# Moving one 512 KB load from ahead of a job's rows to behind its weights

## The chip, the cores and the metric

The kernel runs on one core of a Trainium2 chip. The metric is the device time of one execution in microseconds (us), and several runs are compared by their median. A core has TensorE for matmuls (PE, with PEld for its weight loads), VectorE (DVE), ScalarE (ACT), GpSimd (POOL) and SyncE (SP), which only issues transfers and reads registers. All transfers of the core share 16 DMA engines; those that SP issues go through one queue of the profile (q1), the indirect ones that POOL issues through another (q0).

## The reference

A retention layer (linear attention with a decay per head) over 4 batches of 768 tokens, 8 heads of 64, then a mixture of 8 experts, where each token goes to the one expert with the largest gate value:

```python
for t in range(S):
    state = gamma * state + k[:, :, t] (outer) v[:, :, t]
    y[:, :, t] = scale * q[:, :, t] @ state
x = y as 3072 rows of 512
logits = x @ w_gate + modality_bias[modality_id]
e_idx = argmax(logits); gate_w = softmax(logits)[e_idx]
for e in range(8):                      # 512 -> 1024 -> 512, relu between
    out[rows of e] = gate_w * (relu(x[rows of e] @ w1[e]) @ w2[e])
```

All inputs and the output are float32.

## The kernel before

The retention part is cut into 24 chunks of 128 tokens (`NN`), numbered 0 to 23. A chunk needs two transfers of 512 KB: `kq` (keys and queries by feature, `load_kq`, L114) and `kv` (keys and values by token, `load_kv`, L120). Chunks below `WHOLE = 9` are computed in one piece (`whole_scores`, `whole_state`, `whole_out`), later ones in two halves (`quarters`). For each chunk POOL multiplies the values by decay factors (`decay_v`, L1059, tile `vd`); PE adds keys times `vd` to a running state (`st`; `grown` in the later chunks, all recorded at L276), and forms the output `y` from the scores `sc`. `tokens_out` (L388) then gives the rows `x` of the expert layer and their gate values.

Rows are routed in groups of three chunks. When a group is routed, POOL scatters its rows (`x_dram<-xs,pos`, L494, three indirect transfers, one per chunk) into lists by expert in DRAM. From the lists come jobs: a job is 256 rows of one expert. The kernel begins its first job before most chunks are done: after group 1 (chunks 3, 4 and 5). `start_job` reads the place of the job's rows from a small list (L986), and `load_rows` brings them in as `xg` (L838, two transfers of 257 KB), which wait for the scatters of the groups that may hold the job's rows. PE transposes them (`flip_x`, `xp`, L857), ACT and DVE split them and the weights `raw` into high and low parts (`hi`, `lo`, L813 and L815), and PE multiplies (`h`, L872, then `o`, L887), three products for one. The 10 jobs that begin before the routing is complete have an `e` in their names. The weights of the first job are loaded early for a guessed expert; L809 loads them again only if the guess was wrong, and the second matrix follows at L807.

The order of work on PE, ACT, DVE and SP is that in which the Python code emits it (`manual_schedule`): each engine runs its own instructions in that order and waits where an input or a buffer isn't ready. `retention` is a generator that emits one step at a time, and `everything` puts the jobs' steps between its steps. SP therefore issues its transfers one after the other; one that has to wait holds up all that stand behind it. The pool for `kv` has three buffers beside four borrowed ones: chunk 11 takes the buffer of chunk 8, chunk 12 that of chunk 9.

Of the kernel before, what the change touches and what calls it, by code (L numbers as in the profile page):

```python
# [41 lines left out]
WHOLE = 9  # L42
# [13 lines left out]
def kernel(  # L56
# [43 lines left out]
    def room(kind, n, bufs):  # L100
        shape, name = [P, 2, DM], f"{kind}_{n}"
        if (kind, n) in lent:
            return me.tile(shape, F32, tag=lent[kind, n], name=name)
        if kind == "kq":
            return fours[free.index(n) % 4].rearrange("p (a b) -> p a b", a=2)
        return ld.tile(shape, F32, tag=kind, name=name, bufs=bufs)
# [9 lines left out]
    def load_kv(n):  # L116
        if n in kvs or n >= NN:
            return
        t = kvs[n] = room("kv", n, 3)
        nc.sync.dma_start(t, qkv[n][:, 2:4])  # L120
# [33 lines left out]
    def setup_a():  # L154
        nc.vector.tensor_copy(wgt[:, :, :P], ident.unsqueeze(1).to_broadcast([P, NG, P]))
        nc.vector.memset(ones, 1.0)
        nc.vector.memset(cnt[0], 0.0)
# [53 lines left out]
    def scores(n):  # L211
        p = psc[n] = bank(f"sc_{n}").rearrange("p (u g t) -> p u g t", u=2, g=NG)
        kt, qt = feat(n, 0), feat(n, 1)
        return [
            (p[rows(j), u, g], kt[rows(j), g, rows(u)], qt[rows(j), g, rows(u)], True)
            for u in range(2) for g in range(NG) for j in range(2)
        ]

    def masked(n):
        att[n] = wk.tile([P, 2, NG, D], F32, tag="a", name=f"a_{n}")  # L220
        nc.vector.tensor_tensor(
            att[n].rearrange("p u g t -> p (u g) t"),
            psc.pop(n).rearrange("p u g t -> p (u g) t"),
            half.unsqueeze(1).to_broadcast([P, H, D]), op=ALU.mult,
        )
# [47 lines left out]
    def run(*lists):  # L273
        for i in range(0, max([0] + [len(l) for l in lists]), 2):
            for out_, l, r, start in sum((l[i : i + 2] for l in lists), []):
                nc.tensor.matmul(out_, l, r, start=start, stop=True, skip_group_check=True)  # L276
# [4 lines left out]
    def whole_scores(n):  # L281
        kt, qt = feat(n, 0), feat(n, 1)
        p = [bank(f"sc{j}_{n}").rearrange("p (g t) -> p g t", g=NG) for j in range(2)]
        for g in range(NG):
            for j in range(2):
                nc.tensor.matmul(
                    p[j][:, g], kt[rows(j), g], qt[rows(j), g], start=True, stop=True,
                    skip_group_check=True,
                )
        psc[n] = p  # L290

    def whole_masked(n):
        p = psc.pop(n)
        att[n] = me.tile([P, 2, NG, P], F32, tag=f"hi1{2 + n % 2}", name=f"a_{n}")
        for j in range(2):
            nc.vector.tensor_tensor(
                att[n][:, j], p[j], mask.unsqueeze(1).to_broadcast([P, NG, P]), op=ALU.mult
            )

    def whole_state(n):  # L300
        c = n % NCH
        if c == 0:
            pst[n // NCH] = bank(f"st_{n}")[:, : NG * D].rearrange("p (g e) -> p g e", g=NG)
        p = pst[n // NCH]
        kk = kvs[n][:, 0].rearrange("p (h d) -> p h d", h=H)
        for g in range(NG):
            for j in range(2):
                nc.tensor.matmul(
                    p[rows(j), g], kk[:, 2 * g + j], vds[n][:, 2 * g + j],
                    start=(c == 0 and g == 0), stop=True, skip_group_check=True,  # L310
                )
        keep_state(n + 1, 0)
        if c == NCH - 2 and n + 1 < WHOLE:
            pst.pop(n // NCH)
# [66 lines left out]
    def tokens_out(n, yT):  # L381
        xs = xrows[n] = wk.tile([P, ROW], F32, tag="xs", name=f"xs_{n}", bufs=6)
        lh = wk.tile([P, H, NE], F32, tag="lh", name=f"lh_{n}")
        c = n % NCH
        for u in range(2):
            px = bank(f"x_{n}_{u}")[:, : 2 * XW].rearrange("p (b e) -> p b e", b=2)
            for g in range(2):
                nc.tensor.matmul(  # L388
                    px[:, g], yT[:, 2 * u + g], wgt[:, 2 * u + g], start=(g == 0), stop=(g == 1),
                    skip_group_check=True,  # L390
                )
            hs = slice(4 * u, 4 * u + 4)

            def gained(out_, src, w):
                shape = [P, 2, 2, w]
                nc.vector.tensor_tensor(  # L396
                    out_.rearrange("p (b j) w -> p b j w", b=2),
                    src.rearrange("p b (j w) -> p b j w", j=2),
                    gain[:, c, hs].rearrange("p (b j) -> p b j", b=2).unsqueeze(3)
                    .to_broadcast(shape),  # L400
                    op=ALU.mult,
                )

            gained(lh[:, hs], px[:, :, P:], NE)
            x = xs[:, u * 2 * P : (u + 1) * 2 * P].rearrange("p (h d) -> p h d", h=4)
            if u == 0:
                gained(x, px[:, :, :P], D)
            else:
                for i in range(4):
                    nc.scalar.activation(  # L410
                        x[:, i], px[:, i // 2, rows(i % 2)], AF.Copy,
                        scale=gain[:, c, 4 * u + i : 4 * u + i + 1],
                    )
        gr = n // GRP
        if n % GRP == 0:
            lg[gr] = sm.tile([P, GRP, NE], F32, tag="lg", name=f"lg_{gr}")
        nc.vector.tensor_reduce(
            lg[gr][:, n % GRP], lh.rearrange("p h e -> p e h"), axis=AX.X, op=ALU.add
        )
# [635 lines left out]
    def decay_v(n):  # L1055
        vv = kvs[n][:, 1].rearrange("p (h e) -> p h e", h=H)
        by = decw if n < WHOLE else dec
        vds[n] = wk.tile([P, H, D], F32, tag="vd", name=f"vd_{n}", bufs=3)
        ins = nc.gpsimd.tensor_tensor(  # L1059
            vds[n], vv, by[:, n % NCH].unsqueeze(2).to_broadcast([P, H, D]), op=ALU.mult  # L1060
        )
        vd_last[:] = [getattr(ins, "ins", ins)]
        if held and n >= WHOLE:
            held.pop(0)()
# [88 lines left out]
    def retention(modi):  # L1153
        whole_scores(0)
        whole_masked(0)
        decay_v(1)
        setup_a()
        prev = None
        for n in range(NN):
            if n < WHOLE:  # L1160
                if (n + 1) % NCH:
                    whole_state(n)

                load_kv(n + 7 if n < 3 else n + 3)
                listed = n == (min(EVENTS) + 1) * GRP
                if listed:

                    tokens_out(*prev)
                    route(min(EVENTS))
                if n + 1 < WHOLE:  # L1170
                    whole_scores(n + 1)
                else:
                    run(scores(n + 1))
                    if (n + 1) % NCH:
                        hand_over(n + 1)

                yield n
                if n + 1 < WHOLE:
                    whole_masked(n + 1)
                else:  # L1180
                    masked(n + 1)
                if prev is not None and not listed:
                    tokens_out(*prev)
                    if n % GRP == 0:
                        route(n // GRP - 1)
                if n + 1 == WHOLE:
                    run(grown(n + 1, 0))
                    keep_state(n + 1, 1)
                if not listed:
                    yield n  # L1190
                prev = None
                yT = whole_out(n)
            else:
                yT = yield from quarters(n)
                if n + 1 < NN:
                    masked(n + 1)
                load_kv(n + 3)
            if n + 2 < NN:
                decay_v(n + 2)
            load_kq(n + 8 if n < 4 else n + 4)  # L1200
            if n == 0:
                setup_b(modi)
            elif n == 1:
                list_consts()
            if prev is not None:
                tokens_out(*prev)
                if n % GRP == 0:
                    route(n // GRP - 1)
            prev = (n, yT)
            yield n  # L1210
        tokens_out(*prev)
        route(NGRP - 1)
        yield NN
# [172 lines left out]
```

## Time and profile before

| | us |
|---|---|
| Median of 3 runs | 418.19 (418.08 to 419.0) |
| The profiled execution | 419.12 |
| Its span, first to last instruction | 417.3 |
| PE busy in the span | 398.5 (95%) |
| PE weight loads, DVE, ACT, POOL busy | 349.3, 251.6, 207.3, 90.6 |

The profile shows one execution, instruction by instruction, with times from the span's start; some 1.8 us of the execution lie around the span. Where PE is busy nearly all the time, what counts is the few places where it waits, and the place of any delay: one that PE meets while it has nothing else to do lengthens the program.

### The profile page before, as it was taken

How to read it: one execution, taken by the hardware profiler on the slowest of the kernel's cores; microseconds unless marked ns; L12 is line 12 of the kernel's file. 1: busy time of each engine (PE TensorE's matmuls, PEld its weight loads, DVE VectorE, ACT ScalarE, POOL GpSimd, SP SyncE). 2: the span in 40 equal slices, each digit the busy share in tenths (PEclk: the TensorE clock that was granted, in tenths of full speed). 3: DMA queues.
4: the chain of work that ended last, by engine and by line, in shares of the span. 5: the costliest groups of instructions: out<-in, count | busy, mean ns of one | idle time of the engine just before them, and what ended most of it. 6: DMA issues, size and time to landing. Idle time of an engine off the chain costs nothing.

```text
span 417.3 us, 11996 instructions
## 1 busy us (share of the span) xinstructions
PE 398.5 (95%) x4598; PEld 349.3 (84%) x4598; DVE 251.6 (60%) x605; ACT 207.3 (50%) x420; POOL 90.6 (22%) x118
## 2 busy tenths in 40 slices
PE   3999859999999999999999999999999999999993
PEld 3888759889979988988988988979898998878852
DVE  1777847855654767547855855967665673725600
ACT  1235347456645554556446547536554655536411
POOL 2426310233132124112501231310230101002001
PEclk9999989999999999999999999999999999999998
DMA  8999659979887764536940414842287688998001
GB/s 278 392 413 357 183 161 373 361 255 337 268 294 264 273 229 130 174 91 217 300 134 37 144 50 153 248 157 78 78 276 257 207 276 309 347 409 336 2 2 44
DMA packets 29978, 92.78 MB, mean 222 GB/s; under 512 B 4827, under 2 KB 4955, under 8 KB 29857
## 3 DMA queue, kind: packets, MB, share of 16 engines
q1 hardware_dynamic: 25360, 77.83, 54.3%
q0 software_dynamic: 4272, 13.67, 8.5%
q8 instruction: 37, 0.61, 0.6%
q10 hardware_dynamic: 288, 0.50, 0.4%
q14 instruction: 21, 0.17, 0.1%
HBM read 92.74 MB, written 17.48 MB: 264 GB/s over the span
## 4 chain that ended last, share of the span: by engine, by line
PE 65%; issue 16%; DMA 4%; DVE 2%; POOL 2%; POOLq 1%; ACT 1%; SPq 0%; ACTq 0%
PE h_e L872 25%; PE o_e L887 24%; PE x L388 5%; PE sc L276 3%; PE st L276 3%; PE xp_e L857 2%; PE y L276 2%; DMA x_dram<-xs,pos 2%; POOL out_dram L900 1%; DMA raw<-in_w_dram 1%; DMA xg_e<-x_dram 1%; DVE lo_e L815 1%; DMA four<-in_w_dram 1%; ACT hi_e L813 1%; POOL out_dram L974 0%
## 5 line engine op out<-in xcount | busy, mean ns | idle before, releaser
L815 DVE TENSOR_TENSOR lo_e<-raw,hi_e 128x1024 fp32r<-128x1024 f32 x80 | 100.1, 1253 | 75.9 <-ACT hi_e L813 75.4
L872 PE MATMUL h_e<-xTh,hi_e 128*128 128x256 f32 x320 | 91.9, 287 | 0.0
L872 PE MATMUL h_e<-xTh,lo_e 128*128 128x256 f32 x320 | 90.3, 282 | 0.0
L872 PE MATMUL h_e<-xTl,hi_e 128*128 128x256 f32 x320 | 90.3, 282 | 0.0
L813 ACT CAST hi_e<-raw 128x1024 fp32r<-128x1024 f32 x80 | 83.7, 1047 | 4.4 <-DMA raw<-in_w_dram 4.4
L887 PE MATMUL o_e<-hi_e,hTh 128*128 128x512 f32 x160 | 66.1, 413 | 0.0
L887 PE MATMUL o_e<-lo_e,hTh 128*128 128x512 f32 x160 | 63.2, 395 | 0.0
L887 PE MATMUL o_e<-hi_e,hTl 128*128 128x512 f32 x160 | 63.0, 394 | 0.0
L872 PEld LDWEIGHTS h_e<-xTh,hi_e 128*128 128x128 f32 x320 | 60.7, 190 | 0.7
L872 PEld LDWEIGHTS h_e<-xTh,lo_e 128*128 128x128 f32 x320 | 60.6, 189 | 0.3
L872 PEld LDWEIGHTS h_e<-xTl,hi_e 128*128 128x128 f32 x320 | 60.7, 190 | 0.0
L1059 POOL TENSOR_TENSOR vd<-kv,cst 128x512 f32<-128x512 f32 x24 | 26.3, 1098 | 102.8 <-PE y L276 39.3
L822 ACT ACTIVATE hTh<-h_e 128x256 fp32r<-128x256 f32 x80 | 30.8, 388 | 29.7 <-PE h_e L872 26.1
L410 ACT ACTIVATE xs<-x,cst 128x64 f32<-128x64 f32 x96 | 22.3, 316 | 45.2 <-DVE lh L396 26.6
L900 POOL DMA_INDIRECT out_dram<-o_e,xg_e x20 | 19.8, 988 | 111.2 <-ACT o_e L899 94.9
L823 DVE SCALAR_TENSOR_TENSOR hTl<-h_e,hTh 128x256 fp32r<-128x256 f32 x80 | 33.0, 418 | 13.7 <-ACT hTh L822 13.6
L887 PEld LDWEIGHTS o_e<-lo_e,hTh 128*128 128x128 f32 x160 | 30.1, 188 | 7.0
L887 PEld LDWEIGHTS o_e<-hi_e,hTh 128*128 128x128 f32 x160 | 30.1, 188 | 6.1
L494 POOL DMA_INDIRECT x_dram<-xs,pos x24 | 27.8, 1157 | 34.1 <-DVE xs L460 12.7
L899 ACT ACTIVATE o_e<-o_e,xg_e 128x512 f32<-128x512 f32 x20 | 13.8, 690 | 42.8 <-issue 27.9
L887 PEld LDWEIGHTS o_e<-hi_e,hTl 128*128 128x128 f32 x160 | 30.2, 189 | 5.5
L815 DVE TENSOR_TENSOR lo_s<-raw,hi_s 128x1024 fp32r<-128x1024 f32 x16 | 19.6, 1222 | 21.0 <-ACT hi_s L813 21.0
(214 smaller groups left out, 670.9 us busy)
## 6 DMA issues: line engine op xcount, KB each, us to landing
raw<-in_w_dram SPq DMA_DIRECT2D x100, 512.0 KB
kv<-in_qkv_dram SPq DMA_DIRECT2D x24, 512.0 KB
four<-in_qkv_dram SPq DMA_DIRECT2D x19, 512.0 KB
xg_e<-x_dram SPq DMA_DIRECT2D x20, 257.0 KB
four<-in_w_dram SPq DMA_DIRECT2D x8, 512.0 KB
wb_u<-in_w_dram SPq DMA_DIRECT2D x16, 256.0 KB
kq<-in_qkv_dram SPq DMA_DIRECT2D x4, 512.0 KB
xg_s<-x_dram SPq DMA_DIRECT2D x4, 257.0 KB
```

Of the source, the lines that this page charges most:

```text
L276: nc.tensor.matmul(out_, l, r, start=start, stop=True, skip_group_check=True)
L388: nc.tensor.matmul(px[:, g], yT[:, 2 * u + g], wgt[:, 2 * u + g], start=(g == 0), stop=(g == 1), skip_group_check=True,)
L410: nc.scalar.activation(x[:, i], px[:, i // 2, rows(i % 2)], AF.Copy, scale=gain[:, c, 4 * u + i : 4 * u + i + 1],)
L494: ins = nc.gpsimd.indirect_dma_start(out=x_dram[:, :], out_offset=bass.IndirectOffsetOnAxis(ap=pos[:, i : i + 1], axis=0), in_=xs, in_offs ...
L813: nc.scalar.copy(hi, raws[m][i])
L815: nc.vector.tensor_tensor(lo, raws[m][i], hi.bitcast(F32), op=ALU.subtract)
L822: nc.scalar.activation(hi, src, AF.Relu)
L823: nc.vector.scalar_tensor_tensor(lo, src, 0.0, hi.bitcast(F32), op0=ALU.max, op1=ALU.subtract)
L872: nc.tensor.matmul(ph, s["w1"][f // 2][wi][:, o : o + P], s["xT"][kc // 2][a][:, kc % 2, :], start=(n == 0), stop=(n == 3 * KC - 1),)
L887: nc.tensor.matmul(po, hT[f][a][:, hh * P : (hh + 1) * P], s["w2"][f // 2][wi][:, (f % 2) * DM : (f % 2 + 1) * DM], start=(n == 0), stop=( ...
L900: ins = nc.gpsimd.indirect_dma_start(out=out[:, :], out_offset=bass.IndirectOffsetOnAxis(ap=xg.bitcast(I32)[:, DM : DM + 1], axis=0), in_= ...
L1059: ins = nc.gpsimd.tensor_tensor(vds[n], vv, by[:, n % NCH].unsqueeze(2).to_broadcast([P, H, D]), op=ALU.mult)
```

## The change

```diff
@@ retention, chunks in one piece
-                load_kv(n + 7 if n < 3 else n + 3)
+                if n + 1 < WHOLE:
+                    load_kv(n + 7 if n < 3 else n + 3)
@@ retention, chunks in halves
                 yT = yield from quarters(n)
                 if n + 1 < NN:
                     masked(n + 1)
+
+                if n == WHOLE:
+                    load_kv(n + 2)
                 load_kv(n + 3)
```

With `n = 8` the old code issued the `kv` load of chunk 11 (the twelfth, as they are counted from 0). The new code leaves it out there and issues it with `n = 9`, just ahead of that of chunk 12. In between the code emits the first job's start: the read of its list, its rows and its weights. Nothing else is added or removed.

On SP, around the first job's start, `kv_11` stood ahead of the reads of the list `lst1` and of the job's rows `xg0` and `xg1`; the last number of a name is only a buffer's number, and `e10` is the first job. Before:

```order
L807 DMA raw13_105<-in_w1_dram 128x1024
L120 DMA kv_10_694<-in_qkv_dram 128x1024
L120 DMA kv_11_815<-in_qkv_dram 128x1024
L986 TENSOR_LOAD lst1_850
...
L838 DMA xg0_e10_875<-x_dram_75 128x514
```

After:

```order
L807 DMA raw13_105<-in_w1_dram 128x1024
L120 DMA kv_10_694<-in_qkv_dram 128x1024
L986 TENSOR_LOAD lst1_848
...
L838 DMA xg0_e10_873<-x_dram_75 128x514
```

The load of chunk 11 no longer stands ahead of the rows. Further on in SP's order, behind the first job's second weight matrix (`raw20` to `raw23`), before:

```order
L807 DMA raw23_109<-in_w2_dram 128x1024
L114 DMA four_76<-in_qkv_dram 128x1024
L120 DMA kv_12_1049<-in_qkv_dram 128x1024
L114 DMA four_76<-in_qkv_dram 128x1024
L986 TENSOR_LOAD lst1_850
```

After:

```order
L807 DMA raw23_109<-in_w2_dram 128x1024
L114 DMA four_76<-in_qkv_dram 128x1024
L120 DMA kv_11_1047<-in_qkv_dram 128x1024
L120 DMA kv_12_1049<-in_qkv_dram 128x1024
L114 DMA four_76<-in_qkv_dram 128x1024
L986 TENSOR_LOAD lst1_848
```

It now stands where the load of chunk 12 stood, and that load and all behind it come one transfer later; `four` is the buffer of `kq`.

On POOL, which waits for `kv_11`, the order is the same in both kernels. Here it is in the new one, with the three scatters of group 1 (`pos_1`) ahead of the decays:

```order
L494 DMA x_dram_75<-xs_3_496,pos_1_720 24704x514
L494 DMA x_dram_75<-xs_4_573,pos_1_720 24704x514
L494 DMA x_dram_75<-xs_5_623,pos_1_720 24704x514
L1059 TENSOR_TENSOR vd_10_948<-kv_10_694,cst_77 128x512
L1059 TENSOR_TENSOR vd_11_1051<-kv_11_1047,cst_77 128x512
L1059 TENSOR_TENSOR vd_12_1298<-kv_12_1049,cst_77 128x512
```

`vd_11` keeps its place between `vd_10` and `vd_12`. PE's order is also the same in both; it first uses `vd_11` and `kv_11` in the second half of chunk 10, between two parts of the first job:

```order
L276 MATMUL sc_11_1130<-four_76 64x64 x2
L276 MATMUL y_10_1129<-a_10_1045,vd_10_948 64x64 x2
L276 MATMUL st_9_832<-vd_11_1051,kv_11_1047 64x64 x2
L276 MATMUL y_10_1129<-a_10_1045,vd_10_948 64x64 x2
L276 MATMUL st_9_832<-vd_11_1051,kv_11_1047 64x64 x2
```

Nothing moved there, but its input `kv_11` is now issued later.

## The prediction

> **What bounds the kernel now.** I read first who waits for whom, for PE alone: in the whole run there are three waits that matter.
>
> ```profile
> PE sc L286 <- DMA four<-in_qkv_dram: 5.4, 1, 5.4
> PE xp_e L857 <- DMA xg_e<-x_dram: 4.2, 2, 3.2
> PE st L344 <- ACT s L271: 1.1, 1, 1.1
> ```
>
> The columns are total us, times, longest. The first is the start of the program. The second, 4.2 us, is PE waiting for the rows of the first job. Then the busy time by stretch (length, then busy us of PE, PEld, DVE, ACT, POOL, then PE clock, DMA share, GB/s):
>
> ```profile
> 53.00:63.00 10.00, 5.82 (x109) 5.07 (x102) 5.07 (x9) 4.74 (x10) 0.39 (x1) 0.83 0.59 180
> 63.00:100.00 37.00, 37.00 (x559) 33.24 (x558) 26.12 (x62) 22.46 (x46) 10.09 (x10) 1.00 0.92 325
> ...
> 300.00:400.00 100.00, 100.00 (x692) 86.56 (x691) 55.03 (x75) 52.38 (x83) 11.97 (x12) 1.00 0.72 255
> ```
>
> From 63 to 400 us PE has no gap, so what PE wins by 63 us is kept to the end unless a new wait appears; and what it loses isn't won back. The chain of waits through the gap:
>
> ```profile
> 46.65 6.94 DMA x_dram<-xs,pos
> 53.60 0.35 SPq L838
> ...
> 54.17 3.62 DMA xg_e<-x_dram
> 57.83 1.45 PE xp_e L857 x7
> ```
>
> The third scatter of group 1, issued at 46.65, lands only at 53.60; until then SP can't issue the rows, and these take 3.6 us more. SP had come to that wait at 50.6 (first row), 3.0 us earlier (second row):
>
> ```profile
> L838 SPq MOVE xg_e<-x_dram x2: 29/29/29, 50.6 to 54.1; - x2
> SPq L838 <- DMA x_dram<-xs,pos: 3.0, 1, 3.0
> ```
>
> So the scatter's landing, not SP, sets the end of the gap. The load that moves was issued in the midst of the scatters:
>
> ```profile
> 44.05 1.01 POOL L494 DMA_INDIRECT x_dram<-xs,pos  x1 [2.95 <-DVE key L662]
> 45.37 0.97 POOL L494 DMA_INDIRECT x_dram<-xs,pos  x1 [0.30 <-issue]
> 46.65 0.98 POOL L494 DMA_INDIRECT x_dram<-xs,pos  x1 [0.30 <-issue]
> L120 SPq DMA_DIRECT2D kv<-in_qkv_dram x1: 339/339/339, 45.8 to 45.8; - x1
> 46.50:48.00 1.50, 0.41 (x14) 0.27 (x12) 1.43 (x4) 1.36 (x6) 1.35 (x2) 1.00 1.00 52
> 48.00:49.50 1.50, 1.31 (x23) 1.14 (x24) 1.16 (x5) 0.37 (x1) 0.70 (x1) 1.00 0.75 284
> 49.50:51.00 1.50, 1.50 (x38) 1.34 (x36) 1.34 (x5) 0.35 (x2) 0.00 (x0) 1.00 0.89 354
> 51.00:53.50 2.50, 2.35 (x90) 1.88 (x80) 0.00 (x0) 0.84 (x4) 1.04 (x1) 1.00 0.05 16
> ```
>
> From 46.5 to 49.5 us, 1.5 x 52 + 1.5 x 284 GB/s = 0.50 MB moved: just the 0.52 MB of the load. The next 1.5 us carry 0.53 MB, what two scatters of 257 KB amount to. So scatters two and three went behind the load. The first scatter, ahead of it, landed after 4.4 us; the 24 scatters of the run range from 3.2 to 8.4:
>
> ```profile
> DMA to landing us min/median/max: 4.4/4.4/4.4
> DMA to landing us min/median/max: 3.2/5.9/8.4
> ```
>
> **Gain: the rows come earlier.** One transfer of 512 KB leaves the DMA engines at 46.5 to 49.5 us. By how much the third scatter lands sooner, call it G, no row shows; the bounds are these. From above, SP isn't ready before 50.66, so G is at most 53.60 - 50.66 = 2.94. From below 0, if the landing hangs on something else. Between lie two rows. If the third scatter lands like the first, at 46.65 + 4.4 = 51.05, G is 2.55. If only the time that the load needs at the best rate is saved, 0.524 MB / 418 GB/s (row of 68 to 71 us below), G is 1.25. That lower value has a reason of its own: in this stretch the instruction queue has one packet, and its share is large.
>
> ```profile
> q8 instruction: 1, 0.02, 5.2%
> ```
>
> 5.2% of 16 engines over 46.5 to 50 us is 0.052 x 16 x 3.5 = 2.9 us: one DMA engine was held by one instruction fetch, and its part of the scatters ends last with or without the load. I take the middle of 1.25 and 2.55, G = 1.9.
>
> The Trainium skill, page "DMA: Bandwidth & Descriptors", section "Queues, rings and completion order", says that a DMA engine takes turns between queues by whole packets of some 9 to 17 descriptors; the order of bytes above agrees. The same page, section "Anatomy of one DMA — SWDGE (gpsimd) path", puts the fixed cost at about 2.0 us and adds bytes at 436 GB/s, an estimate of 2.6 us for a scatter; the trace has 4.4 at its place, and by the page's figure the rows would wait only for SP (G = 2.94).
>
> **Cost: chunk 11 comes later.** The load now stands where that of chunk 12 stood, the sixth of those that SP issues without condition behind the rows (four of weights, one `kq`), and the wait moves to POOL's `vd`:
>
> ```profile
> 52.35 1.04 POOL L1059 TENSOR_TENSOR vd<-kv,cst 128x512 f32<-128x512 f32 x1 [3.65 <-PE y L328]
> 70.59 1.04 POOL L1059 TENSOR_TENSOR vd<-kv,cst 128x512 f32<-128x512 f32 x1 [17.20 <-DMA kv<-in_qkv_dram]
> 58.11 1.95 SPq L807 DMA_DIRECT2D raw<-in_w_dram  x4
> 60.15 0.52 SPq L114 DMA_DIRECT2D four<-in_qkv_dram  x1
> 60.78 0.40 SPq L120 DMA_DIRECT2D kv<-in_qkv_dram  x1
> 71.49 0.23 PE L276 MATMUL st<-vd,kv 64*64 64x64 f32 x2
> ```
>
> The first row is `vd_11`, done at 53.4, 18 us before PE uses it at 71.49 (last row). The second is `vd_12`, which begins at 70.59, when its load, issued at 60.78, has landed. In the new kernel `vd_11` takes that place: SP's whole sequence from the rows on is earlier by G, so it begins at 70.59 - G and ends 1.04 later; with 0.1 for the signal PE can go on at 71.73 - G. Without this wait PE would come there at 71.49 - G or sooner. So this costs at least 0.24, and whatever PE wins above G there is lost again. All other engines only follow.
>
> PE can win above G, since its clock fell:
>
> ```profile
> 58.00:59.20 1.20, 1.20 (x7) 0.88 (x6) 0.93 (x2) 1.20 (x3) 0.00 (x0) 0.58 0.07 10
> 59.20:62.30 3.10, 3.10 (x72) 2.98 (x72) 2.75 (x6) 1.65 (x4) 0.00 (x0) 0.61 0.97 330
> ...
> 68.00:71.00 3.00, 3.00 (x30) 2.87 (x28) 1.87 (x9) 1.70 (x3) 0.41 (x1) 1.00 1.03 418
> ```
>
> The granted clock is about 0.6 here and 1.00 in the last row: 1.2 x 0.42 + 3.1 x 0.39 = 1.7 us of PE time lost, of which I count 1.3 as winnable, since ACT and DVE, which split the rows, then set the pace. It would bring PE to the `st` row at 71.49 - G - 1.3, where it waits 1.54 for `vd_11`. So I cost it at nothing in the sum, and it is the cover for a `kv_11` that lands earlier than I think.
>
> The other moves I cost at nothing. SP's 0.4 us for the issue go from one place where SP waits later (3.0 us at the rows) to one ahead of the second job's loads. Chunk 12's load comes one transfer, 1.25 us, later, so `vd_12` at some 73 - G; PE uses it after 83.63. The second job's rows and weights come 1.25 later too; its rows, issued from 70.45 on, take 9.5 us at most, till 81.2, and PE wants them at 88.69. POOL has no work between the two `vd`, so nothing queues behind the waiting `vd_11` but `vd_12`.
>
> ```profile
> 70.45 1.56 SPq L838 DMA_DIRECT2D xg_e<-x_dram  x2
> DMA to landing us min/median/max: 2.7/3.2/9.5
> 83.63 0.20 PE st L276 x2
> 88.69 0.87 PE xp_e L857 x8
> ```
>
> **The sum.** -1.9 + 0.24 = -1.7 us: 417.4 against the profiled execution's 419.12. That execution is 0.93 above the median, so against the median 418.19 it is 416.5. With G at 1.25 and 2.55 the same sum gives 417.2 and 415.9.
>
> **Rivals.** First, the scatter lands when it did: it writes rows to DRAM, one DMA engine is held by the instruction fetch anyway, and other scatters took up to 8.4 us. Then G is 0, the 0.24 stays, and the time is 418.4. Against it stands the order of the bytes. Second, on the other side: `kv_11` lands late. The place is PE's `st` at 71.49, and it decides once the load lands more than 0.6 us later than chunk 12's did, against G = 0 (with 0.24, 0.84 in all). If G is 0 and it lands one transfer later, the price is 0.24 + 1.25 = 1.5, the time 419.7. For it speaks that DMA ran at 330 GB/s from 59.2 to 62.3, well under 418, so landing times move; against it, that any G must be used up first. Third, more gain: the clock doesn't fall and `kv_11` comes sooner than its predecessor did, as the same 330 against 418 allows (3.1 us at 418 would carry 0.27 MB more, 0.65 us). With G at 2.55 and all of the 1.3, it is 418.19 - 3.85 = 414.3. The Trainium skill, page "TensorE: Matmul & The Clock Gate", section "What's actually happening", has the clock fall after an idle window of some 3.4 us; the trace agrees, with a fall some 5 us after PE ran dry, and a gap shortened by 2 us would by that rule likely not make it fall.
>
> **How the numbers follow.** Chances: the forecast 0.55, no gain in the scatter 0.20, `kv_11` late 0.10, more gain 0.15. A difference under 0.2% (0.84 us) is about what can't be told from no change. Of the forecast's share nearly all lies beyond it (G above 1.1), of which I give 0.02 to the second group: faster 0.68, same 0.22, slower 0.10. The range leaves out the late load and the far end of the third rival: 414.4 to 418.4.
>
> **What the profile after would show.** The third scatter lands at 50 to 52.4 us instead of 53.60, and the stretch from 46.5 carries scatters. SP's wait at the rows is under 2 us. PE's wait for the rows falls from 4.2 to about 2.3 or less, and the clock stays at 1.00. New is a PE wait for `vd` (L1059) of 0.2 to 1.6 us in the second half of chunk 10, at 68 to 70, with POOL's wait for `kv` ending there twice in a row. PE has no other new wait after it. Wrong would be a landing still near 53.6; a PE wait for `vd` longer than what the gap lost; or a new PE wait for the second job's rows.

## The result and the profile after

| | before | after |
|---|---|---|
| Median of six runs each, us | 418.15 (417.44 to 419.0) | 415.94 (414.53 to 416.36) |
| The profiled execution, us | 419.12 | 415.21 |
| Its span, us, and mean granted clock | 417.3, 0.991 | 413.4, 0.998 |

The ratio is 0.994, with a 95% interval of 0.9922 to 0.9958: 2.2 us faster by the medians, 3.9 by the two profiled executions, of which the one of before is 1.0 above its median and the one of after 0.7 below. All of after's times must be read with a shift: its first scatter of group 1 is issued at 43.38 instead of 44.05, so 0.67 us of the 3.9 was won ahead of anything that the change touches.

The chain of waits of after, through the same place (start, us, what):

```profile
45.97 4.12 DMA x_dram<-xs,pos
50.11 0.34 SPq L838
...
50.65 2.85 DMA xg_e<-x_dram
53.55 0.98 PE xp_e L857 x7
...
56.85 8.72 DMA kv<-in_qkv_dram
...
65.71 1.78 POOL vd L1059
67.53 0.27 PE st L276 x2
```

The third scatter takes 4.12 us to land instead of 6.94, the rows 2.85 instead of 3.62, and PE begins `xp` at 53.55 instead of 57.83.

Which transfer went first can be read from the packets by queue (packets, MB, share of the 16 engines; q1 is SP's queue, q0 that of the scatters, and a scatter has 80 packets). In before, from 46.7 to 49.3 us and from 49.3 to 52.6:

```profile
q1 hardware_dynamic: 99, 0.41, 86.0%
...
q0 software_dynamic: 160, 0.53, 40.8%
```

In the first of these stretches there is no packet of a scatter at all, only the load and one fetch of instructions; the second holds all 160 packets of scatters two and three. In after, from 46 to 50 us, they have the engines to themselves beside two fetches of instructions, one of them on q8:

```profile
q0 software_dynamic: 160, 0.53, 35.7%
q8 instruction: 1, 0.02, 2.9%
```

Then something new stands in the chain of after: the moved load, 8.72 us from issue to landing, and behind it `vd_11`. The waits of SP and of PE in after (total us, times, longest):

```profile
SPq L838 <- DMA x_dram<-xs,pos: 0.2, 1, 0.2
```

```profile
PE st L276 <- POOL vd L1059: 1.5, 1, 1.5
PE st L344 <- ACT s L271: 1.1, 1, 1.1
PE xp_e L857 <- DMA xg_e<-x_dram: 0.6, 2, 0.3
```

SP's wait for the scatter fell from 3.0 to 0.2 us and PE's wait for the rows from 4.2 to 0.6; PE's wait of 1.5 us for `vd_11` is new. The busy time by stretch in after (columns as in the prediction) around those two places:

```profile
53.50:58.00 4.50, 4.45 (x90) 4.21 (x91) 4.24 (x7) 3.19 (x7) 0.00 (x0) 1.00 0.65 199
58.00:62.00 4.00, 4.00 (x90) 3.80 (x88) 2.79 (x9) 3.65 (x10) 0.00 (x0) 1.00 1.03 391
64.00:68.00 4.00, 2.47 (x74) 2.20 (x74) 3.84 (x8) 2.64 (x4) 2.29 (x2) 1.00 1.03 417
```

PE is busy from 53.5 on and the clock stays at 1.00; where PE waits (64 to 68), the DMA engines move 417 GB/s. What SP issued ahead of `kv_11`, the second weight matrix among it, goes first. PE reaches its first `st` on `vd_11` at 67.53 instead of 71.49, 4.0 us earlier, and the results of all later jobs are 3.9 us earlier up to the end. So the whole effect of the change lies between 44 and 68 us: a gain at the rows, part of it given back at `vd_11`.

### The profile page after: what moved, and what is told of

It reads as the page before. It is cut to its first block, busy times and chain, and to the rows that moved or that the text cites. A ratio compares the mean times of both kernels' runs of the same rounds, so it can differ in the third digit from the quotient of the medians.

```text
span 413.4 us, 11999 instructions
## 1 busy us (share of the span) xinstructions
PE 396.7 (96%) x4598; PEld 347.6 (84%) x4598; DVE 252.8 (61%) x605; ACT 207.1 (50%) x420; POOL 91.9 (22%) x118
## 4 chain that ended last, share of the span: by engine, by line
PE 63%; issue 16%; DMA 5%; DVE 3%; POOL 2%; ACT 1%; POOLq 1%; SPq 1%; ACTq 0%
PE o_e L887 24%; PE h_e L872 24%; PE x L388 5%; PE st L276 3%; PE sc L276 3%; PE xp_e L857 2%; DMA kv<-in_qkv_dram 2%; PE y L276 2%; POOL out_dram L900 1%; DMA x_dram<-xs,pos 1%; DVE lo_e L815 1%; ACT hi_e L813 1%; DMA four<-in_w_dram 1%; DMA xg_e<-x_dram 1%; DMA raw<-in_w_dram 1%
## 5 line engine op out<-in xcount | busy, mean ns | idle before, releaser
L815 DVE TENSOR_TENSOR lo_e<-raw,hi_e 128x1024 fp32r<-128x1024 f32 x80 | 102.0, 1276 | 71.0 <-ACT hi_e L813 70.9
L1059 POOL TENSOR_TENSOR vd<-kv,cst 128x512 f32<-128x512 f32 x24 | 28.0, 1170 | 97.2 <-DMA kv<-in_qkv_dram 41.5
```

The lines of the kernel that those rows point to most:

```text
L815: nc.vector.tensor_tensor(lo, raws[m][i], hi.bitcast(F32), op=ALU.subtract)
L1059: ins = nc.gpsimd.tensor_tensor(vds[n], vv, by[:, n % NCH].unsqueeze(2).to_broadcast([P, H, D]), op=ALU.mult)
```

## The experiments

The theory, A: the change does two things that don't depend on each other. It takes 512 KB out of the way of scatters two and three, which helps if the load would have stood there; and it makes `kv_11` late, which costs PE 1.5 us in any case. Its rivals are named with each run. The later runs were on three chips, which the record numbers 1, 14 and 15, four kernels to a chip, each chip with its own runs of the kernel before (medians 415.58, 415.69 and 415.89). For the first comparison the record gives no chip, so that a difference between chips lies behind what follows is likely, but not shown.

**The load between the two weights (chip 1).** As the changed kernel, but `kv_11` is issued after the first matrix of the first job, ahead of the second:

```diff
                     raw(job, 1, guess)
+                    load_kv(WHOLE + 2)
                     raw(job, 2)
```

> The load of chunk 11 stands between the first job's first and second weight matrix, one to four transfers earlier than in the changed kernel, and behind the rows. My theory: the gain comes from the scatters, which are as free as in the changed kernel, and 1.5 us of it are lost again at PE's wait for vd_11. Here kv_11 lands some 4 us sooner, that wait is gone, and the time is 1.3 to 1.8 us under the changed kernel's 415.94, at about 414.4 (ratio to before 0.990 to 0.992). Rival: the second weight matrix, now one transfer later, makes ACT wait at its first cut, and nothing is won: 415.9 or more (0.994 or above).

Measured: 415.74 us, ratio 0.9997 [0.9981, 1.0012]. Its profile has no wait for `vd_11` and 0.3 us for the rows, as A says, but the time is no better than before: here the kernel before was itself at 415.58, 2.6 us under the first comparison. The gain that A expected was not there to be had.

**The load twice (chip 1).** The old place is kept and the load repeated at the new one, so that both of A's effects should show:

```diff
+                if n == WHOLE:
+                    nc.sync.dma_start(kvs[n + 2], qkv[n + 2][:, 2:4])
```

> Chunk 11 is loaded twice, in the old place and again in the new one, and vd_11 waits for the second load. My theory: the old place slows the scatters whatever is done later, so the third scatter lands near 53.6 us again (6 to 7 us after issue), PE's clock falls again, and the later load costs its 0.2 us or a little more: 418.2 to 419.2 (ratio 1.000 to 1.003). Rival: the gain comes from the later place (the order of the loads behind the rows), and the early transfer is hidden: near 416 (0.994 to 0.996).

Measured: 417.94 us, 1.005 [1.0032, 1.0068]. PE's wait for `vd` is 1.5 us, but the scatters are not late: the early load was issued at 46.56, behind the third scatter's 44.58, and the rows at 49.52. The late scatter that was expected isn't there in this profile, which leaves the new place's cost alone. It is the fastest of the eight executions (416.29; five are above 417.5), so what the longer ones did is not shown.

**A small load early (chip 1).** 32 KB of `kv_11` in the old place, all of it in the new:

```diff
+                    t = kvs[n + 3] = room("kv", n + 3, 3)
+                    nc.sync.dma_start(t[:, 0, :64], qkv[n + 3][:, 2, :64])
```

> As the changed kernel, but in the old place stands a load of 32 KB (a sixteenth of the transfer, with the same waits on SP); the whole of chunk 11 is loaded in the new place. My theory: what slows the scatters is the time that 512 KB take in the DMA engines, so this behaves as the changed kernel: third scatter 4 to 5 us from issue to landing, 415.7 to 416.5 (ratio 0.994 to 0.996). Rival: it is SP's wait for chunk 8 at that place, or that any transfer is issued among the scatters at all: 418 (0.999 to 1.001).

Measured: 418.12 us, 1.0058 [1.0039, 1.0078], again with 1.5 us for `vd`. On the same chip the whole 512 KB in the old place (417.94) cost no more than 32 KB: by the medians, the load was in nobody's way there.

**Work for PE in the gap (chip 1).** The kernel before, with four matmuls of 128 x 472 that nobody needs ahead of `flip_x`, to ask whether the fall of the clock was part of the loss:

> The kernel before, with four matmuls of 128x472 (some 3.2 us) that nothing reads, put on PE ahead of the first job's transposes, into the gap. The load of chunk 11 stays in the old place. My theory: the rows come as late as before, but the clock stays at 1.00, which gives back up to 1.7 us of PE time, 1.3 of it after ACT and DVE: 416.5 to 417.2 (ratio 0.996 to 0.998). Rival: the fall of the clock costs nothing, because ACT and DVE set the pace behind the rows: 418.2 (1.000).

Measured: 417.93 us, 1.0059 [1.0036, 1.0082]. The clock was at 1.00, but here the rows were on time (SP waited 0.3 us for the scatter), so there was no gap to fill and the matmuls (3.4 us in the chain) only delayed PE. Whether the fall of the clock was part of the loss stays open.

After these four it was open whether the first comparison or its reading was at fault.

**The two kernels again, and two places for the load (chip 14).** `e5_before` and `e6_after` are the two kernels unchanged, `e7_between` is the first experiment again, and `e8_behind_rows` puts the load directly behind the first job's rows:

```diff
         if j is jobs[0]:
             rows_in(s)
+            load_kv(WHOLE + 2)
```

> The kernel before, unchanged, for its profile on the chip of these runs (the four runs before this one were compared with a median of 415.58, not 418.15). Theory A: where the time before is about 415.6, the load of chunk 11 is issued after or well apart from the third scatter, the scatter lands within 5 us, PE's wait for the rows is under 1 us and the clock stays at 1.00; where it is about 418.2, all is as in the profile shown (landing 6 to 7 us, PE's wait over 3 us). Theory B: the difference between 418.2 and 415.6 has nothing to do with this place; then the landing is 6 to 7 us at 415.6 as well.

> The changed kernel, unchanged. Theory A: it meets a PE wait for vd_11 of 1.5 us in any case. Where the time before is about 418.2, it is faster as before (ratio 0.993 to 0.996). Where it is about 415.6, there is no late scatter to win back and the wait is the whole effect: 417.1 to 418.2, ratio 1.003 to 1.006. Theory B: the ratio is 0.994 here too.

> The load of chunk 11 between the first and second weight matrix, as in the first of the four runs. Theory A: no late scatter and no wait for vd_11, so about 415 to 416 whatever the time before is: ratio 0.990 to 0.995 beside 418.2, 0.998 to 1.001 beside 415.6, and 1.5 us or more under the changed kernel of this call. Theory B: no faster than the changed kernel.

> The load of chunk 11 directly behind the job's two row transfers, ahead of the read of the expert's number and of all weights. Theory A: as the place between the weights, within 0.5 us of it; SP's 0.4 us for the issue delay the first weight cut on ACT by as much, and PE behind it by at most 0.4. Rival: in that place it delays the rows or the cuts by its whole transfer of 1.25 us: 1.0 to 1.5 us above the place between the weights.

| | us | ratio to before |
|---|---|---|
| before again | 416.34 | 1.001 [0.9997, 1.0024] |
| after again | 417.94 | 1.0049 [1.0031, 1.0067] |
| between the weights | 415.64 | 0.9995 [0.998, 1.0011] |
| behind the rows | 416.04 | 1.0009 [0.9996, 1.0021] |

The same changed kernel is about 2 us slower than the same kernel before on this chip. The chain of the kernel before here:

```profile
45.78 5.01 DMA x_dram<-xs,pos
...
51.37 2.99 DMA xg_e<-x_dram
```

Its waits on PE, and where SP issued `kv_11` and the rows:

```profile
PE xp_e L857 <- DMA xg_e<-x_dram: 0.7, 2, 0.4
```

```profile
47.67 0.34 SPq L120 DMA_DIRECT2D kv<-in_qkv_dram  x1
50.81 0.90 SPq L838 DMA_DIRECT2D xg_e<-x_dram  x2
```

`kv_11` was issued at 47.67, 1.9 us behind the issue of the third scatter (45.78). In the first comparison it was 45.83, between the second (45.37) and the third (46.65). So the scatter lands after 5.01 us instead of 6.94, PE waits 0.7 us for rows instead of 4.2, and there is no loss for the change to take away.

Why SP was free to issue it so late can be read in part. Four engines (ACT, DVE, POOL and SP) are released together, at 47.44 to 47.67 us, just as PE goes on after two stops that end on nothing the profile shows ("issue"):

```profile
47.41 0.90 PE L276 MATMUL sc<-four 64*64 64x64 f32 x22 [0.41 <-issue]
47.49 0.31 DVE L672 TENSOR_SCALAR gt<-pk,key 96x96 f32<-96x96 f32 x1 [2.01 <-remote]
47.50 1.04 POOL L1059 TENSOR_TENSOR vd<-kv,cst 128x512 f32<-128x512 f32 x1 [0.74 <-remote]
```

DVE's `gt` needs PE's `pk`, whose matmuls had ended at 45.0. The same wait of 2.0 to 2.1 us at `gt` is in ten of the fourteen profiles, all ten from the later runs; neither profile of the first comparison has it, nor PE's stops. That PE's signals were held up there is a guess.

The cost of the change is there all the same; after on this chip, by its chain and PE's waits:

```profile
57.43 9.50 DMA kv<-in_qkv_dram
...
67.07 1.20 POOL vd L1059
```

```profile
PE st L276 <- POOL vd L1059: 1.5, 1, 1.5
```

Between the weights that wait is gone, and 2.3 us with it (417.94 to 415.64). This is A's second half, shown; the wait accounts for 1.5 of the 2.3, and the rest has no cause shown. Behind the rows is 0.4 us more than between, about what A expected and about what these intervals can tell apart.

**The collision made by hand (chip 15).** What was missing is the first half, a load that goes ahead of the scatters (a collision, for short), brought about at will. The kernel is "between", with a load of 512 KB that nobody needs, into the buffer of a weight that is loaded later; it waits for DVE's `key`, which also releases the first scatter:

```diff
+        if t == min(EVENTS):
+            nc.vector.tensor_copy(raws[2][0][:1, 0:1], key[:1])
+            nc.sync.dma_start(raws[2][0], w2[0:1, 0].rearrange("o p f -> p (o f)"))
```

A second kernel issues the same load after DVE's `rank`, behind the third scatter:

```diff
+        if g == min(EVENTS):
+            nc.vector.tensor_copy(raws[2][0][:1, 0:1], rank[:1])
+            nc.sync.dma_start(raws[2][0], w2[0:1, 0].rearrange("o p f -> p (o f)"))
```

> kv_11 is loaded between the first job's two weights, as in e7_between; added is one load of 512 KB that nobody needs (a quarter of an expert's second weight, loaded again later), which SP issues as soon as DVE has written `key` (L658/L662), so at about 44.9 us: some 0.4 us behind the issue of group 1's second scatter and ahead of the third, where the first chip's kernel before had kv_11 (45.83 against 45.37). A (a transfer of 512 KB that enters the DMA engines just ahead of scatters two and three is what made them late in the first comparison): the third scatter takes 6.5 to 7.5 us from issue to landing instead of the 5.0 of e5_before, SP waits 1.5 to 3.5 us for it, the rows are issued at 52.5 to 54 and PE waits 2.0 to 4.5 us for them; the time is 2 to 4 us over between, ratio 1.004 to 1.010. B (on this chip the transfer costs nothing, the first chip's lateness had another cause, its earlier clock or its reads): third scatter at most 5.3 us, PE's wait for rows under 1 us, ratio 0.998 to 1.002.

> The same kernel with the same extra load of 512 KB, issued behind DVE's `rank` (L674), so at 47.1 to 47.5 us, after all three scatters are issued (45.8) and where e5_before had kv_11 (47.7). A: the scatters are ahead of it in the DMA engines, the third takes 5.0 to 5.5 us, PE waits under 1.2 us for rows, ratio 0.998 to 1.003, so 2 us or more under e9_collide. B: as e9_collide within 0.5 us. C (any extra 512 KB in these microseconds costs the rows about as much, whenever it starts): both alike, both over 1.004.

Measured: 416.89 us, 1.0031 [1.0005, 1.0056] ahead of the scatters; 416.22 us, 1.0036 [1.0006, 1.0065] behind them. Neither median decides, because the executions of both spread widely: of the twelve with the load ahead, eight lie between 415.1 and 417.0, one is 417.9, and three lie between 420.2 and 420.5. One of those three (420.53) is the profiled one. In it the load was issued at 44.08, earlier than expected: 0.34 us behind the first scatter (43.74) and ahead of the second (45.05). All three went behind it all the same: from 43 to 46.9 us only q1 has packets, and from 47 to 52 q0 has 240, three times 80:

```profile
q0 software_dynamic: 240, 0.79, 40.8%
```

Its chain (from the inserted lines on, its line numbers are 3 higher than those of the kernel before):

```profile
39.77 1.08 DVE crep L643
...
46.33 5.98 DMA x_dram<-xs,pos
52.33 0.35 SPq L841
...
52.89 4.67 DMA xg_e<-x_dram
...
57.60 1.71 PE xp_e L860 x7
```

Its wait on PE, and its stretches:

```profile
PE xp_e L860 <- DMA xg_e<-x_dram: 3.6, 2, 2.1
```

```profile
53.50:57.50 4.00, 0.47 (x13) 0.17 (x5) 1.83 (x2) 2.81 (x5) 0.00 (x0) 1.00 0.48 150
...
58.00:61.00 3.00, 3.00 (x71) 2.67 (x69) 1.84 (x4) 1.17 (x2) 1.04 (x1) 0.50 0.83 289
```

This resembles the kernel before of the first comparison: the scatter late, PE without work, `xp` begun at 57.6 (57.8 there), and then the clock at 0.50 for 3 us. The first job's results come out at 87.8 us, against 88.0 there and 82.7 in "between" of the same chip (84.7 in `e7_between`, which had the same order of `crep` and `vd`, see below). So the collision can cost what the first comparison showed. But three executions of twelve took that long; what happened in the others no profile shows. The expected 6.5 to 7.5 us of landing was 5.98 and SP's wait 1.4 (1.5 to 3.5 expected), with the rest of the delay in the rows' own transfer (4.67 instead of 2.78 in "between").

And the late load, which A held to be harmless, spread as widely: five of its twelve lie between 417.7 and 420.8. Its profiled execution was one of the others (416.35, rows issued at 50.69, PE waiting 0.6 us). The five have a mean granted clock of 0.992 to 0.994, the other seven 0.995 to 0.999; with the load ahead, the four longest have 0.993 or 0.994 and the others 0.995 or more. So in both kernels the longest executions are those with a lower clock, as in the profiled one (0.993). What lowered it in the five is not shown. The rival C, that both cost alike, has the medians on its side, though neither reaches the 1.004 that it named.

**Both versions once more (chip 15).**

> The changed kernel, nothing else. A: which sign it shows depends on whether the kernel before meets the collision on this chip. If before's median is near 418.2 (first chip): 0.993 to 0.996. If it is near 415.6: 1.003 to 1.006, with PE waiting 1.5 us for vd of chunk 11. B (the first comparison's gain holds everywhere and the two later ones were disturbed): 0.992 to 0.996 whatever before's median.

> kv_11 loaded between the first job's two weights, nothing else. A: it meets neither the collision nor the wait for vd: 0.998 to 1.001 where before is near 415.6, 0.990 to 0.993 where before is near 418.2; in both cases under e11_after by 0.5 to 2.5 us. B: equal to e11_after within 0.4 us.

Measured: after 417.92 us, 1.0044 [1.0027, 1.0061]; between 415.72 us, 0.9999 [0.9984, 1.0015]. Both are A's numbers for a chip whose kernel before is near 415.6. B, by which the gain of the first comparison holds everywhere, has fallen: on both chips where the two kernels ran later, the change loses 0.4 to 0.5%.

**What goes with the collision.** One pair of rows differs between the profiles with a collision and most others. Here is DVE's `crep` and POOL's `vd` (chunk 9) just ahead of the scatters, in the first comparison's kernel before, and in the kernel before on chip 14:

```profile
40.13 1.04 DVE L643 COPY crep<-cnt 128x96 bf16<-128x96 bf16 x1
40.06 1.04 POOL L1059 TENSOR_TENSOR vd<-kv,cst 128x512 f32<-128x512 f32 x1 [0.71 <-PE y L328]
```

```profile
40.10 0.21 DVE L643 COPY crep<-cnt 128x96 bf16<-128x96 bf16 x1
40.11 1.10 POOL L1059 TENSOR_TENSOR vd<-kv,cst 128x512 f32<-128x512 f32 x1 [0.80 <-PE y L328]
```

The two start within 0.1 us of each other, and `crep` takes 1.04 us or 0.21. Where it takes 0.21, POOL waits 1.0 us less for `key` and the scatters go earlier:

| profiled execution | `crep`, us | POOL's wait for `key`, us | the 512 KB issued, against the third scatter | PE's wait for rows, us | time |
|---|---|---|---|---|---|
| before, first comparison | 1.04 | 2.95 | 0.8 ahead | 4.2 | 419.12 |
| load ahead of the scatters, by hand | 1.08 | 2.94 | 2.3 ahead | 3.6 | 420.53 |
| after, first comparison | 1.06 | 2.95 | none | 0.6 | 415.21 |
| between, chip 14 | 1.10 | 2.95 | none | none | 417.58 |
| before, chip 14 | 0.21 | 1.98 | 1.9 behind | 0.7 | 416.24 |
| load twice | 0.21 | 1.98 | 2.0 behind | 0.3 | 416.29 |
| load behind the scatters, by hand | 0.21 | 1.98 | 2.5 behind | 0.6 | 416.35 |

All seven other profiles have 0.21. Both rows in which PE waits long for the rows have the long `crep` and the load ahead; the two with the long `crep` and no load among the scatters don't have that wait. So the long `crep` alone doesn't make the rows late. It isn't free of loss either: the profiled execution of "between" on chip 14 is the longest of twelve, 1.9 us over their median, and its clock fell without any wait for rows:

```profile
45.20:48.60 3.40, 2.35 (x49) 1.81 (x48) 3.30 (x9) 1.48 (x7) 2.78 (x4) 1.00 0.48 179
48.70:52.00 3.30, 3.28 (x29) 2.94 (x28) 1.69 (x7) 0.62 (x2) 0.25 (x1) 0.50 0.15 55
```

What the load ahead of the scatters does with the short `crep` no profile shows, so whether it takes both is open.

## Why the prediction was right, and where it was not

**What bounds the kernel.** That the third scatter's landing set the end of the gap, and that PE keeps to the end what it wins by 63 us, held: from the first job on, every job's results moved by the same 3.9 us.

**The gain G.** It was taken as 1.9, the middle of 1.25 and 2.55, under a bound of 2.94. It is 6.94 - 4.12 = 2.82. The step that was mis-sized is the lower row, by which only 1.25 us of the load would be saved, since the one DMA engine held by an instruction fetch would end last anyway. The load held the engines for twice as long: no packet of a scatter moves from 46.7 to 49.3. The prediction's own row had this (46.5 to 48 us, the engines' share at 1.00 for 52 GB/s); 418 GB/s was the rate of another stretch. An instruction fetch is there in after as well (2.9% of 16 engines over 4 us, 1.9 us of one engine), and the third scatter landed after 4.12, somewhat sooner than the first one had in before (4.4), which was the upper row's reading. Beside G the rows' own transfer became 0.77 us shorter (3.62 to 2.85), a term that the sum didn't have.

**The clock.** It was costed at nothing, with 1.3 us as winnable. It stayed at 1.00, so this gain was made; it went into the cover for `kv_11`, as the prediction said it would. The kernel before had PE busy 0.30 us of the 4.20 ahead of the fall, and the kernel with the collision by hand 0.47 of 4.00; both fell to 0.50 for 3.0 to 3.4 us. In before:

```profile
53.60:57.80 4.20, 0.30 (x1) 0.14 (x1) 0.52 (x1) 1.60 (x4) 0.00 (x0) 1.00 0.50 127
58.20:61.60 3.40, 3.40 (x72) 2.95 (x71) 3.13 (x5) 2.10 (x6) 0.00 (x0) 0.50 0.71 233
```

After, PE never stood idle so long. The Trainium skill, page "TensorE: Matmul & The Clock Gate", section "What's actually happening", gives half speed after an idle window of about 3.4 us. These two traces agree. The one of "between" on chip 14 differs: its clock fell to 0.50 at 48.6 us, though PE had been busy 2.35 of the 3.40 us before, with stops of at most 0.4 us. So that a gap is short doesn't by itself keep the clock up.

**The cost at `vd_11`.** Put at 0.24 in the sum, 0.2 to 1.6 as a wait, it was 1.5 us as a wait, from 66.0 to 67.5 us and not at 68 to 70. The larger G and the clock brought PE there sooner. In after, `vd_11` itself took 1.78 us instead of 1.04, which the sum didn't foresee:

```profile
65.35 1.23 DVE L815 TENSOR_TENSOR lo_e<-raw,hi_e 128x1024 fp32r<-128x1024 f32 x1
```

DVE's `lo_e` was in progress when `vd_11` began at 65.71, and ended at 66.58; the last 0.91 us of `vd_11` follow. That is so in all five profiles with this wait (both of the changed kernel on the later chips, the load twice, the small load early, and this one): `vd_11` begins while `lo_e` runs and ends 0.91 or 0.92 us behind it, and PE's wait is 1.5 us in each, although `vd_11` begins anywhere from 0.3 us before to 0.3 us after PE is ready for it. So the late load brings `vd_11` into `lo_e`, and `lo_e` sets the length of the wait. The Trainium skill, page "SBUF — State Buffer", section "SBUF: two separate sides", says that GpSimd excludes a VectorE instruction that has two inputs in SBUF, or that runs in a mode with two ports, and that whichever starts first keeps the shared ports to its end. The rows here agree with the first case. `crep` is a copy with one input; its rows look like the second case, but no row shows its mode.

**The sum.** It gave -1.7 us, and the medians -2.2. The net at PE's `st` is 3.96 less the start's 0.67, so 3.3 us: 2.8 at the scatter, 0.8 at the rows, 0.5 in the faster `xp` (1.45 to 0.98), and the rest of the clock, less 1.5 of waiting. The two errors, a gain and a cost both too small, partly cancel: that the sum came within 0.5 us of the medians is in part luck.

**The rivals.** No gain in the scatter (418.4) and `kv_11` late (419.7, that is +1.5 over before) did not happen in the first comparison. In the later runs both did: there is no gain to be had at the scatter, because the load isn't in the way, and the kernel is about 2 us slower than before. The third, more gain (414.3), came in part in the first comparison: the clock didn't fall, and `vd_11` began 8.9 us after the issue of its load (56.85 to 65.71), where `vd_12` had begun after 9.8 (60.78 to 70.59); PE's wait took most of that back. The prediction weighed whether the landing hangs on the load, and gave that it might not 0.2. It did not ask whether the load would stand there in every execution: its issue lay 0.46 us behind one scatter's and 0.82 ahead of the next's. That margin could be read from the rows that the prediction quotes. What the rows couldn't tell is that SP may be released for the load two microseconds later, as on chip 14.

## What to carry to other kernels

A transfer of 512 KB issued ahead of small scatters, or even 0.3 to 0.5 us behind one, goes before them here and can make the step late that waits for their landing. But read the margin of the order before counting a gain: a difference of a microsecond or two between runs of the same kernel puts the load on the other side. A load moved out of the way should be moved no further than needed: behind the rows but ahead of 2 MB of weights it was 2.2 to 2.3 us better than behind them, and on none of the three chips told apart from before. Beside the first comparison it wasn't run; without the 1.5 us of waiting, 414.4 is the estimate for it. And one comparison, with a tight interval, doesn't tell the sign of a change that rests on such a margin.

## What was not expected of the hardware

The kernel before runs at 418.15 us in the first comparison and at 415.58, 415.69 and 415.89 on chips 1, 14 and 15, over 81 runs of which none was above 417.4; the change is 0.994 in the first and 1.0049 and 1.0044 on chips 14 and 15. Neither sign is scatter of the measurement: all of these intervals exclude 1.

One DVE copy of 128 x 96 takes 0.21 or 1.04 to 1.10 us, and with it three scatters move by a microsecond. In all fourteen profiles it begins within 0.07 us of POOL's `vd`. It is long in four in which `vd` began 0.01 to 0.07 us ahead, and short in nine in which `vd` began with it or behind it. In the last (after on chip 15) the rows have `vd` 0.01 us ahead (40.30 against 40.31) and the copy is short.

Two things stay open. In the kernel before on chip 14, SP is released for `kv_11` only at 47.67 us, though PE's `st` of chunk 8 (L308), which reads the buffer that the load takes, ended by 45.6. And from the first job's first result to the second job's first, all twelve profiles of the later runs take 34.2 to 34.7 us, both of the first comparison 32.5. Of these 1.7 to 2.2 us, 1.0 to 1.1 are time in which PE stands still, mostly in stops of 0.4 us that end on nothing the profile shows.
